# Layer norm and MLP on one core: two token tiles turned by VectorE instead of one, and a narrower first wave of matmuls

## The chip, the cores and the metric

The kernel runs on one core of a Trainium2 chip. A core has five engines that run their own instruction streams and wait for each other by semaphores: TensorE (PE; its weight loads are listed as PEld), VectorE (DVE), ScalarE (ACT), GpSimd (POOL) and SyncE (SP), which here only issues transfers. Tiles lie in the on-chip memory with 128 partitions; matmul results go to eight banks of PSUM, each with 512 float32 columns. The metric is the device time of one execution in microseconds (us), the median of several.

## What is computed

`x` is 2048 tokens by 1024 features, `w1` is 1024 by 3584, `w2` is 3584 by 1024, all in bfloat16:

```
B, S, D, F = 1, 2048, 1024, 3584
y = _layernorm(x, axis=-1)                      # (x - mean) / sqrt(var + eps)
h = _gelu(jnp.einsum("bsd,df->bsf", y, w1) + b1)
return jnp.einsum("bsf,fd->bsd", h, w2) + b2
```

## The kernel before

The tokens are worked on in four blocks of 512, each of four tiles of 128 tokens. For a block, the first product (`mm1`) has 28 rows: row `r` is 128 of the 3584 hidden features, accumulated in one PSUM bank over eight steps `dt` of 128 features, each a matmul of a 128x128 piece of `w1` against 512 token columns of `yT_sb`, the transposed normalized tokens. ACT applies the gelu and writes `hT_sb`. The second product (`mm2`) takes 28 steps for each of its chunks of 512 output columns. A matmul of 512 columns takes 0.216 us, and there are 896 for `mm1` and 896 for `mm2`.

The change is in the start of block 0, while `x` and `w1` arrive. There the first `R = 8` rows of `mm1` are opened early, all eight banks at once, in a "wave": each of the 64 (row, dt) pairs is a cell, one matmul with the piece of `w1` that is there by then. Tiles 0, 1 and 2 are called `RAW`: they go into the wave as they came, not normalized. PE transposes them (`pe_T`, L320 to L356, against an identity), ACT copies the result out of PSUM into buffer 0 of `yT_sb` (L352), and two columns of ones beside them (`N_ONES`) give the column sums of `w1`. ACT copies the negated sums to `ncs` (`put_cs`, L573). Later `ops_fix` (L533) corrects each of the eight rows in PSUM: L536 adds the mean of each token times the column sum, L539 multiplies by the reciprocal standard deviation. For that, means and deviations have to lie along the free dimension: DVE turns them (`ops_row_turn`, L475, L480) and ACT spreads them from the first 32 partitions to the other three groups (`put_row_spread`, L486). `ops_centre` (L523, L529) subtracts the means from the three raw tiles into buffer 1 of `yT_sb`, in four pieces of two `dt`; from row 8 on the matmuls of 512 columns use buffer 1, and only the scaling is left to DVE (L423).

Tile 3 takes another way. DVE takes its statistics (L248, L258), POOL raises the variance to the power -1/2 (L255), DVE normalizes (L262) and transposes it in blocks of 32x32 into `xq_sb` (L490, 1.25 us). Sixteen blocks of 32 partitions then have to move to their places: three by DVE (L498), four by POOL (L495), nine by ACT (L507, `put_moves_3`). Its 64 cells of 128 columns run after the raw wave, row by row; the first waits for all moves, and for the column sums of its row, which its columns overwrite.

The order on each engine is fixed by the order in which the program is written. On DVE it is: statistics of tiles 0, 1, 2; half of the turning of the means; statistics of tile 3; the rest of the turning; normalize, transpose and move tile 3; turn the deviations; centre pieces 0 and 1; fix rows 0 and 1; centre pieces 2 and 3; fix rows 2 to 7. On ACT: copies of the transposed tiles, spreading of the means, column sums of rows in banks 0 to 3, moves of tile 3, two of three spreading copies of the deviations, the other column sums, the last spreading copy, then the gelus. Row 8 reuses the bank of row 0, so it waits for that row's gelu. After the start a planner orders DVE's work for the next blocks by estimated times.

SP issues the loads in one queue in the order of `SP_FIRST_LOADS`. `PIECES` cuts the first 1024 columns of `w1` into nine loads: `(j0, j1, rows)` is the steps `j0` to `j1` for those rows. Rows 0 to 3 come first for all `dt`, then rows 4 to 7; every line of a load is 512 columns, 1024 bytes.

Of the kernel before, what the change touches and what calls it, by code (L numbers as in the profile page):

```python
# [92 lines left out]
def bass_standalone__mixer_channel_mlp__prompt_kernel(  # L93
# [49 lines left out]
    with ExitStack() as es:  # L143
# [176 lines left out]
        def pe_T(i, groups, banks):  # L320
            blk = i // TPB
            src_ev = y_ev[i] if i in y_ev else [x_ev[i][0]] * DT
            evs = yT_ev.setdefault(i, [None] * DT)
            prev = None
            for k, (g0, g1) in enumerate(zip(groups[:-1], groups[1:])):
                bname = banks[k]
                for j in range(g0, g1):
# [8 lines left out]
                    pe.op(lambda e, i=i, j=j, o=off, bap=bank_of[bname]: e.transpose(  # L336
                        out=bap[:, o:o + P], in_=x_sb[:, i, j * P:(j + 1) * P], identity=ident[:, :]),
                        waits=waits, sig=(f"tp{i}_{k}" if last else None))
# [2 lines left out]
            off = 0
            prev = None
            for k, (g0, g1) in enumerate(zip(groups[:-1], groups[1:])):
                bname = banks[k]
                if bname != prev:
                    off = 0
                prev = bname
                done = max(m for m in range(len(banks)) if banks[m] == bname)
                src = bank_of[bname][:, off:off + (g1 - g0) * P].bitcast(I32)
                src = src.rearrange("p (j s) -> p j s", j=g1 - g0)  # L350
                dst = yT_sb[:, 0 if i in RAW else ybuf(blk), g0:g1, ycol(i):ycol(i) + P].bitcast(I32)
                act.op(lambda e, dst=dst, src=src: e.copy(out=dst, in_=src), waits=[f"tp{i}_{done}"],  # L352
                       sig=f"te{i}_{k}")
                off += (g1 - g0) * P
                bank_read[bname] = f"te{i}_{k}"
# [119 lines left out]
        def ops_row_turn(k):  # L475
            res = []
            for tq in range(4):
                src = stat_r[32 * tq:32 * (tq + 1), :, 2 * k:2 * k + 1].to_broadcast([32, len(RAW), 32])
                dst = row_b(k)[0:32, :, 32 * tq:32 * (tq + 1)]
                res.append((lambda e, src=src, dst=dst: e.transpose(out=dst, in_=src),  # L480
                            [("rstd" if k else "mv") + str(t) for t in RAW], (f"row_q{k}" if tq == 3 else None), 0.22))
            return res

        def put_row_spread(k, q0, q1):
            for q in range(q0, q1):
                act.op(lambda e, q=q: e.copy(out=row_b(k)[32 * q:32 * (q + 1)], in_=row_b(k)[0:32]),  # L486
                       waits=[f"row_q{k}"], sig=(f"row_{k}" if q == 3 else None))

        def moves_3():
            res = [(lambda e: e.transpose(out=xq_sb[:, :], in_=x_sb[:, 3, :]), [y_ev[3][-1]], "xq", 1.07)]  # L490
            for tq, q in POOL_MOVES + DVE_MOVES:
                src = xq_sb[32 * tq:32 * (tq + 1), :].rearrange("p (j q s) -> p j q s", j=DT, q=4)[:, :, q, :].bitcast(I32)
                dst = yT_sb[32 * q:32 * (q + 1), ybuf(0), :, ycol(3) + 32 * tq:ycol(3) + 32 * (tq + 1)].bitcast(I32)
                if (tq, q) in POOL_MOVES:
                    pool.op(lambda e, src=src, dst=dst: e.tensor_copy(out=dst, in_=src), waits=["xq"],  # L495
                            sig=("tg3" if (tq, q) == POOL_MOVES[-1] else None))
                if (tq, q) in DVE_MOVES:
                    res.append((lambda e, src=src, dst=dst: e.tensor_copy(out=dst, in_=src), ["xq"],  # L498
                                ("tc3" if len(res) == len(DVE_MOVES) else None), 0.2))
# [2 lines left out]
        def put_moves_3():
            todo = [(tq, q) for tq in range(4) for q in range(4) if (tq, q) not in DVE_MOVES + POOL_MOVES]
            for tq, q in todo:
                src = xq_sb[32 * tq:32 * (tq + 1), :].rearrange("p (j q s) -> p j q s", j=DT, q=4)[:, :, q, :].bitcast(I32)
                dst = yT_sb[32 * q:32 * (q + 1), ybuf(0), :, ycol(3) + 32 * tq:ycol(3) + 32 * (tq + 1)].bitcast(I32)
                act.op(lambda e, src=src, dst=dst: e.copy(out=dst, in_=src), waits=["xq"],  # L507
                       sig=("te3" if (tq, q) == todo[-1] else None))
            yT_ev[3] = ["te3"] * DT
# [42 lines left out]
        pe_T(0, GROUPS_0, ("t", "2_0"))  # L552
        pe_T(1, GROUPS_0, ("2_1", "1_4"))
        pe_T(2, GROUPS_2, ("t", "2_0"))
        put_row_spread(0, 1, 4)
# [8 lines left out]
        first = [(r, dt) for r in PIECES[0][2] for dt in range(*PIECES[0][:2])]  # L564
        for tiles in (RAW[:2], RAW[2:]):
            for r, dt in first:
                wave_cell(r, dt, tiles)
        cells = [(r, dt) for j0, j1, rows in PIECES[1:] for r in rows if r < R for dt in range(j0, j1)]
        for n, (r, dt) in enumerate(cells):
            wave_cell(r, dt, RAW, f"raw_{r}" if dt == DT - 1 else None)  # L570
# [9 lines left out]
        put_cs(0, 4, ps_1[:, 0:4, one0:one0 + 1])  # L580
        put_moves_3()
        put_row_spread(1, 1, 3)
        put_cs(4, NB1, ps_1[:, 4:NB1, one0:one0 + 1])
# [110 lines left out]
```

## Time and profile before

| | |
|---|---|
| median of 3 runs | 396.38 us (396.07, 396.38, 396.78) |
| the profiled execution | 396.67 us, its span 395.4 us |
| PE busy | 390.9 us, 99% of the span |
| DVE, ACT, POOL busy | 162.0, 86.2, 11.7 us |
| transpositions on PE for block 0 | 24, from 3.71 to 6.38 us |
| raw wave, 8 rows by 8 dt | 6.38 to 16.84 us |
| cells of tile 3 | 16.84 to 20.42 us |
| matmuls of 512 columns | from 20.42 us |

Times inside the profile count from the span's first instruction. A line of the timeline gives the start and the duration in us, the engine, the line of the program, the operation, what it writes and reads, how many were merged, and in brackets the idle time before it with what ended it. A matmul is listed from its start until its result is in PSUM, so consecutive ones overlap; the distance of their starts, called the pitch here, is what counts for PE's time. SPq lines are the issue of a transfer, and the view of transfers gives the time from that issue to the landing.

### The profile page before, as it was taken

The numbers are of one execution on the slowest core, as the hardware profiler recorded it, in microseconds if no ns is written. First come the engines' busy times: TensorE is split into PE (matmuls) and PEld (weight loads), VectorE is DVE, ScalarE is ACT, GpSimd is POOL, SyncE is SP. The second block draws the span as 40 slices with busy tenths as digits, with TensorE's granted clock in tenths as the row PEclk, the third lists the DMA queues.
The fourth block names the chain that finished last, engine by engine and source line by source line (L and its number), as shares of the span: only waits on it lengthen the run. The fifth ranks groups of instructions, "written<-read, shape, count | busy, mean of one in ns | idle before, by whom it ended". The sixth has DMA issues, their size and how long they took to land.

```text
span 395.4 us, 4518 instructions
## 1 busy us (share of the span) xinstructions
PE 390.9 (99%) x1904; PEld 184.9 (47%) x1938; DVE 162.0 (41%) x338; ACT 86.2 (22%) x139; POOL 11.7 (3%) x59
## 2 busy tenths in 40 slices
PE   9999999999999999999999999999999999999998
PEld 7744444444444444444444444444444444444444
DVE  5998889988999306987100000001100000001011
ACT  3655420000144332000023443100003334400000
POOL 3101000011001100000000000000000000000000
DMA  7999940000000000000000000000000000000000
GB/s 257 373 385 386 387 155 26 16 27 14 28 0 0 2 0 0 28 26 15 28 13 2 0 0 2 13 13 28 25 15 15 0 0 2 0 15 27 13 28 27
DMA packets 16078, 23.63 MB, mean 60 GB/s; under 512 B 1082, under 2 KB 8250, under 8 KB 16058
## 3 DMA queue, kind: packets, MB, share of 16 engines
q1 hardware_dynamic: 16016, 23.33, 16.7%
q8 instruction: 15, 0.25, 0.3%
q14 instruction: 5, 0.04, 0.0%
q10 hardware_dynamic: 42, 0.01, 0.0%
HBM read 19.14 MB, written 4.19 MB: 59 GB/s over the span
## 4 chain that ended last, share of the span: by engine, by line
PE 99%; issue 0%; DVE 0%
PE ps L449 49%; PE ps L382 38%; PE ps_t L382 7%; PE ps L397 3%; PE ps L471 1%; PE ps_t L397 0%; PE ps L336 0%; PE ps_t L336 0%; DVE o_sb L460 0%; PE ps L512 0%
## 5 line engine op out<-in xcount | busy, mean ns | idle before, releaser
L449 PE MATMUL ps<-w_sb,hT_sb 128*128 128x512 bf16 (+2 forms) x909 | 193.3, 373 | 0.8
L382 PE MATMUL ps<-yT_sb,w_sb 128*128 128x512 bf16 x678 | 152.4, 379 | 0.9
L449 PEld LDWEIGHTS ps<-w_sb,hT_sb 128*128 128x128 bf16 x924 | 88.6, 98 | 105.2
L407 ACT ACTIVATE hT_sb<-ps,b_sb 128x512 bf16<-128x512 f32 x94 | 64.0, 687 | 234.4 <-PE ps L382 217.2
L382 PEld LDWEIGHTS ps<-yT_sb,w_sb 128*128 128x128 bf16 x696 | 68.0, 98 | 81.9
L460 DVE TENSOR_TENSOR o_sb<-ps,b_sb 128x512 bf16<-128x512 f32 (+2 forms) x33 | 22.3, 675 | 198.7 <-PE ps L449 198.5
L304 DVE STREAM_TRANSPOSE yT_sb<-x_sb 32x256 bf16<-32x256 bf16 x192 | 83.7, 436 | 21.9 <-PE ps_t L382 18.8
L382 PE MATMUL ps_t<-yT_sb,w_sb 128*128 128x512 bf16 x135 | 31.9, 379 | 0.1
L248 DVE BATCH_NORM_STATS2 st_sb<-x_sb 128x6 f32<-128x512 bf16 x32 | 21.0, 672 | 4.7 <-DMA x_sb<-in_x_dram 4.6
L382 PEld LDWEIGHTS ps_t<-yT_sb,w_sb 128*128 128x128 bf16 x136 | 13.3, 98 | 16.1
L407 ACT ACTIVATE hT_sb<-ps_t,b_sb 128x512 bf16<-128x512 f32 x18 | 12.4, 687 | 17.5 <-PE ps_t L382 14.6
L397 PE MATMUL ps<-yT_sb,w_sb 128*128 128x128 bf16 (+2 forms) x116 | 13.1, 269 | 0.0
L397 PEld LDWEIGHTS ps<-yT_sb,w_sb 128*128 128x128 bf16 x116 | 8.9, 98 | 3.5
L255 POOL TENSOR_TENSOR rstd_sb<-mv_sb,nhalf 128x1 f32<-128x1 f32 x13 | 7.1, 548 | 113.6 <-DVE mv_sb L258 113.6
L423 DVE TENSOR_TENSOR ps<-ps,row_r 128x384 f32<-128x384 f32 x17 | 9.2, 561 | 2.7 <-PE ps L382 2.5
L262 DVE TENSOR_SCALAR x_sb<-x_sb,mv_sb,rstd_sb 128x1024 bf16<-128x1024 bf16 x13 | 7.0, 541 | 2.0 <-POOL rstd_sb L255 1.3
L536 DVE SCALAR_TENSOR_TENSOR ps<-row_r,ncs,ps 128x384 f32<-128x384 f32 x7 | 4.2, 614 | 0.6 <-PE ps L397 0.6
L486 ACT COPY row_r<-row_r 32x384 f32<-32x384 f32 x6 | 3.1, 510 | 4.3 <-DVE row_r L480 4.2
L539 DVE TENSOR_TENSOR ps<-ps,row_r 128x384 f32<-128x384 f32 x7 | 3.9, 563 | 0.2
L529 DVE TENSOR_TENSOR yT_sb<-yT_sb,row_r 128x768 bf16<-128x768 bf16 x4 | 3.6, 950 | 0.0
L471 PE MATMUL ps<-const-bfloat16-1.0 128*128 128x128 bf16 x25 | 2.8, 309 | 0.8 <-PEq L679 0.8
L258 DVE BATCH_NORM_AGGREGATE mv_sb<-st_sb 128x2 f32<-128x15 f32 x13 | 2.9, 222 | 0.4
(34 smaller groups left out, 32.9 us busy)
## 6 DMA issues: line engine op xcount, KB each, us to landing
w_sb<-in_w_dram SPq DMA_DIRECT2D x4, 1792.0 KB, 18.3
w_sb<-in_w_dram SPq DMA_DIRECT2D x2, 2048.0 KB, 16.4
out_dram<-o_sb SPq DMA_DIRECT2D x31, 128.0 KB, 1.7
x_sb<-in_x_dram SPq DMA_DIRECT2D x3, 1024.0 KB, 14.4
w_sb<-in_w_dram SPq DMA_DIRECT2D x7, 256.0 KB, 5.4
x_sb<-in_x_dram SPq DMA_DIRECT2D x4, 256.0 KB, 3.4
w_sb<-in_w_dram SPq DMA_DIRECT2D x1, 1024.0 KB, 10.1
w_sb<-in_w_dram SPq DMA_DIRECT2D x2, 128.0 KB, 3.7
```

What stands on the lines that cost most here:

```text
L248: return (lambda e, i=i, h=h, pw=pw: e.bn_stats(st_sb[i][:, 6 * h:6 * (h + 1)], x_sb[:, i, h * pw:(h + 1) * pw]), [x_ev[i][h if len(x_ev[i ...
L255: pool.op(lambda e, i=i, dst=dst, mv=mv: e.tensor_tensor(out=dst, in0=mv[:, 1:2], in1=nhalf[:, i:i + 1], op=ALU.pow), waits=[f"mv{i}", "nh ...
L262: return (lambda e, i=i, c0=c0, c1=c1: e.tensor_scalar(out=x_sb[:, i, c0:c1], in0=x_sb[:, i, c0:c1], scalar1=mv_sb[:, i, 0:1], scalar2=rst ...
L304: res.append((lambda e, src=src, dst=dst: e.transpose(out=dst, in_=src), waits, (f"tr{i}" if lastop else None), 0.47))
L382: pe.op(lambda e, b=b, r=r, dt=dt, bank=bank: e.matmul(unit_bank(bank)[:, 0:TB], lhsT=w1_sb[:, dt, r * P:(r + 1) * P], rhs=yT_sb[:, ybuf(b ...
L397: pe.op(lambda e: e.matmul(unit_bank(bank)[:, n0:n1], lhsT=w1_sb[:, dt, r * P:(r + 1) * P], rhs=yT_sb[:, 0 if tiles[0] in RAW else ybuf(0) ...
L407: act.op(lambda e, r=r, n0=n0, n1=n1, bank=bank: e.activation(out=hT_sb[:, r, n0:n1], in_=unit_bank(bank)[:, n0:n1], func=ACT.Gelu_apprx_tanh,
L423: crit.append((est[sig], (lambda e, reg=reg: e.tensor_tensor(out=reg, in0=reg, in1=row_b(1), op=ALU.mult), [sig, "row_1"], ready, 0.57), 0))
L449: pe.op(lambda e, sl=sl, ft=ft, c0=c0, c1=c1, bank=bank: e.matmul(ps_2[:, bank, 0:c1 - c0], lhsT=hT_sb[:, ft, sl * P:(sl + 1) * P], rhs=w2 ...
L460: crit.append((est[sig], (lambda e, ob=ob, c0=c0, c1=c1, bank=bank: e.tensor_tensor(out=o_sb[:, ob, c0:c1], in0=ps_2[:, bank, 0:c1 - c0], ...
L471: pe.op(lambda e: e.matmul(ps_1[:, 0, 0:P], lhsT=ones, rhs=ones, start=True, stop=True))
L536: return [(lambda e: e.scalar_tensor_tensor(out=reg, in0=row_b(0), scalar=ncs[:, c:c + 1], in1=reg, op0=ALU.mult, op1=ALU.add), [f"m1_0_{r ...
```

## The change

- `RAW` is now tiles 0 and 1, and the wave's cells are 258 columns wide (256 and the two of ones). PE transposes 16 pieces, not 24, and each tile's transposed pieces go to two banks of their own, cut after `dt` 1 (`GROUPS`).
- Tiles 2 and 3 (`MADE`) both go the way of tile 3. `xq_sb` has a place for each. Tile 2: DVE moves 1 block, POOL 5, ACT 10. Tile 3: DVE 3, POOL 6, ACT 7. POOL's power for tile 3 waits for POOL's moves of tile 2.
- The 64 raw cells are followed by 64 cells of tile 2 and 64 of tile 3, each of 128 columns. A row's first cell in either waits for its column sums.
- `PIECES` loads `w1` by `dt`: for `dt` 0 rows 0 to 3 and rows 4 to 7 apart, then one load of all eight rows for each `dt`, with 2048 bytes to the line. The wave goes through them in the same order. `x3` is loaded after `w4`, not after `w3`, in loads that are still nine and as large.
- On DVE the order is: statistics of tiles 0 and 2, half of those of tile 1, normalize, transpose and move tile 2, statistics of tile 3, the rest of tile 1, normalize, transpose and move tile 3, turn means and deviations together (4 instructions, not 8), centre pieces 0 and 1, then fix row 0, fix row 1, centre pieces 2 and 3, fix the rest.
- On ACT: copies of the transposed tiles, moves of tile 2, five column-sum copies (there were four), moves of tile 3, spreading of the means, spreading of the deviations, gelus.
- What works on raw tiles (L423, L529, L536, L539, spreading copies) has 256 token columns instead of 384.

```diff
-RAW = (0, 1, 2)
+RAW = (0, 1)
+MADE = (2, 3)
-GROUPS_0 = (0, 4, 8)
-GROUPS_2 = (0, 2, 8)
+GROUPS = (0, 2, 8)
-PIECES = ((0, 1, (0, 1, 2, 3)), (1, 2, (0, 1, 2, 3)), (2, 4, (0, 1, 2, 3)), (4, 6, (0, 1, 2, 3)), (6, 8, (0, 1, 2, 3)),
-          (0, 2, (4, 5, 6, 7)), (2, 4, (4, 5, 6, 7)), (4, 6, (4, 5, 6, 7)), (6, 8, (4, 5, 6, 7)))
+PIECES = ((0, 1, (0, 1, 2, 3)), (0, 1, (4, 5, 6, 7))) + tuple((j, j + 1, tuple(range(8))) for j in range(1, 8))
-DVE_MOVES = ((0, 0), (1, 1), (2, 2))
-POOL_MOVES = ((3, 3), (0, 1), (1, 2), (2, 3))
+POOL_MOVES = {2: 5, 3: 6}
+DVE_MOVES = {2: 1, 3: 3}
-SP_FIRST_LOADS = ("b1", "x0", "x1", "x2", "w0", "w1", "w2", "w3", "x3", "w4", "w5", "w6", "w7", "w8")
+SP_FIRST_LOADS = ("b1", "x0", "x1", "x2", "w0", "w1", "w2", "w3", "w4", "x3", "w5", "w6", "w7", "w8")
...
-                    waits=[f"mv{i}", "nhalf"], sig=f"rstd{i}")
+                    waits=[f"mv{i}", "nhalf"] + ["tg2"] * (i == MADE[1]), sig=f"rstd{i}")
...
+        def ops_moves(i):
+            xq = xq_sb[:, i - MADE[0], :]
+            res = [(lambda e: e.transpose(out=xq, in_=x_sb[:, i, :]), [y_ev[i][-1]], f"xq{i}", 1.25)]
+            np_, nd = POOL_MOVES[i], DVE_MOVES[i]
+            for n, (tq, q) in enumerate(quarters[:np_ + nd]):
+                src, dst = move_aps(i, tq, q)
+                if n < np_:
+                    pool.op(lambda e, src=src, dst=dst: e.tensor_copy(out=dst, in_=src), waits=[f"xq{i}"] + ["rstd1"] * (i == MADE[1]),
+                            sig=(f"tg{i}" if n == np_ - 1 else None))
+                else:
+                    res.append((lambda e, src=src, dst=dst: e.tensor_copy(out=dst, in_=src), [f"xq{i}"],
+                                (f"tc{i}" if n == np_ + nd - 1 else None), 0.23))
...
-        seq = st[0] + st[1] + st[2] + turn_m[:2] + st[3] + turn_m[2:] + nm[3] + moves_3() + turn_r + ctr[:2]
-        for o in seq:
+        for o in st0 + st2 + st1[:1] + nm2 + mv2 + st3 + st1[1:] + nm3 + mv3 + ops_row_turn() + ctr[:2]:
             dve_put(o)
...
+        for j0, j1, rows in PIECES:
+            for r in rows:
+                for dt in range(j0, j1):
+                    wave_cell(r, dt, RAW, f"raw_{r}" if dt == DT - 1 else None)
+        put_moves(2)
...
+        for a, b in ((0, 2), (2, 4), (4, NB1)):
+            put_cs(a, b, ps_1[:, a:b, one0:one0 + 1])
         put_cs(NB1, NB1 + NB2, ps_2[:, 0:NB2, one0:one0 + 1])
         put_cs(NB1 + NB2, R, ps_tf[:, one0:one0 + 1].unsqueeze(1))
+        put_moves(3)
+        put_row_spread(0)
+        put_row_spread(1)
         fixes = []
+        for t in MADE:
+            for r in range(R):
+                for dt in range(DT):
+                    pe_wave(r, dt, (t,), wave[r][0], [cs_ev[r], f"tc{t}", f"tg{t}"] if dt == 0 else [],
+                            f"m1_0_{r}" if t == MADE[-1] and dt == DT - 1 else None)
...
-        for o in [a0, a1, b0, b1_] + ctr[2:] + [o for f in fixes[2:] for o in f]:
+        for o in [a0, b0, a1, b1_] + ctr[2:] + [o for f in fixes[2:] for o in f]:
```

More of the change, by code (lines that the diff above doesn't have):

```diff
@@ L117, in bass_standalone__mixer_channel_mlp__prompt_kernel @@
     assert NB1 + NB2 + 1 <= 8 and NB2 == 2
-    assert all(c[-1] == DT for c in (GROUPS_0, GROUPS_2, HALVES))
-    assert TPB == 4 and RAW == (0, 1, 2)
+    assert all(c[-1] == DT for c in (GROUPS, HALVES))
+    assert TPB == 4 and RAW + MADE == (0, 1, 2, 3)
     w1_chunks = [(j0, j1, rows[0] * P, (rows[-1] + 1) * P) for j0, j1, rows in PIECES]
@@ L159, in bass_standalone__mixer_channel_mlp__prompt_kernel @@
         row_r = sb("row_r", [P, 2 * len(RAW), P], F32)
-        xq_sb = sb("xq_sb", [P, D], BF16)
+        xq_sb = sb("xq_sb", [P, len(MADE), D], BF16)
         ncs = sb("ncs", [P, R], F32)
@@ L340, in pe_T, with put_copy @@
                     off += P
[L341 to L355, printed above, removed]
-            pe_t[0] += DT * 0.056
+            pe_t[0] += DT * 0.056
+        def put_copy(i, groups, banks, k):
+            g0, g1 = groups[k:k + 2]
+            bname = banks[k]
+            assert banks.count(bname) == 1
+            src = bank_of[bname][:, 0:(g1 - g0) * P].bitcast(I32)
+            src = src.rearrange("p (j s) -> p j s", j=g1 - g0)
+            dst = yT_sb[:, 0, g0:g1, ycol(i):ycol(i) + P].bitcast(I32)
+            act.op(lambda e, dst=dst, src=src: e.copy(out=dst, in_=src), waits=[f"tp{i}_{k}"], sig=f"te{i}_{k}")
+            bank_read[bname] = f"te{i}_{k}"
         unit_n = [0]
@@ L389, in pe_wave @@
         def pe_wave(r, dt, tiles, bank, waits, sig):
-            raw = tiles[0] == 0
-            base = raw_at if tiles[0] in RAW else 0
+            raw = tiles == RAW
             y0 = ycol(tiles[0]) - (N_ONES if raw else 0)
-            n0 = base + y0 - ycol(RAW[0]) if tiles[0] in RAW else 0
+            n0 = one0 if raw else (tiles[0] - MADE[0]) * P
             n1 = n0 + ycol(tiles[-1]) + P - y0
@@ L397, in pe_wave @@
             pe.op(lambda e: e.matmul(
-                unit_bank(bank)[:, n0:n1], lhsT=w1_sb[:, dt, r * P:(r + 1) * P], rhs=yT_sb[:, 0 if tiles[0] in RAW else ybuf(0), dt, y0:y0 + n1 - n0],
-                start=(dt == 0 and tiles[0] in (0, 3)), stop=(dt == DT - 1), skip_group_check=True),
+                unit_bank(bank)[:, n0:n1], lhsT=w1_sb[:, dt, r * P:(r + 1) * P], rhs=yT_sb[:, 0 if raw else ybuf(0), dt, y0:y0 + n1 - n0],
+                start=(dt == 0), stop=(dt == DT - 1), skip_group_check=True),
                 waits=w, sig=sig)
@@ L473, in bass_standalone__mixer_channel_mlp__prompt_kernel, with ops_row_turn @@
         warm(N_WARM)
-        def ops_row_turn(k):
+        flat = stat_r[:, :, :].rearrange("p t (k two) -> p (t k) two", two=2)[:, :, 0:1]
+        def ops_row_turn():
             res = []
             for tq in range(4):
[L478 to L481, printed above, removed]
-            return res
@@ L484, in put_row_spread @@
-        def put_row_spread(k, q0, q1):
-            for q in range(q0, q1):
+                src = flat[32 * tq:32 * (tq + 1), :, :].to_broadcast([32, 2 * len(RAW), 32])
+                dst = row_r[0:32, :, 32 * tq:32 * (tq + 1)]
+                res.append((lambda e, src=src, dst=dst: e.transpose(out=dst, in_=src), [f"rstd{t}" for t in RAW],
+                            ("row_q" if tq == 3 else None), 0.31))
+            return res
+        def put_row_spread(k):
+            for q in range(1, 4):
@@ L486, in put_row_spread @@
                 act.op(lambda e, q=q: e.copy(out=row_b(k)[32 * q:32 * (q + 1)], in_=row_b(k)[0:32]),
[L487 to L499, printed above, removed]
-            return res
@@ L502, in put_moves_3 @@
[L502 to L509, printed above, removed]
+                       waits=["row_q"], sig=(f"row_{k}" if q == 3 else None))
@@ new lines, in bass_standalone__mixer_channel_mlp__prompt_kernel, with move_aps @@
+        quarters = [(tq, q) for q in range(4) for tq in range(4)]
+        def move_aps(i, tq, q):
+            src = xq_sb[32 * tq:32 * (tq + 1), i - MADE[0], :].rearrange("p (j q s) -> p j q s", j=DT, q=4)[:, :, q, :].bitcast(I32)
+            dst = yT_sb[32 * q:32 * (q + 1), ybuf(0), :, ycol(i) + 32 * tq:ycol(i) + 32 * (tq + 1)].bitcast(I32)
+            return src, dst
+        def ops_moves(i):
[10 more added lines that the diff above has]
+                                (f"tc{i}" if n == np_ + nd - 1 else None), 0.23))
+            return res
@@ L511, in pe_b1, with put_moves @@
+        def put_moves(i):
+            for tq, q in quarters[POOL_MOVES[i] + DVE_MOVES[i]:]:
+                src, dst = move_aps(i, tq, q)
+                act.op(lambda e, src=src, dst=dst: e.copy(out=dst, in_=src), waits=[f"xq{i}"],
+                       sig=(f"te{i}" if (tq, q) == quarters[-1] else None))
+            yT_ev[i] = [f"te{i}"] * DT
         def pe_b1():
@@ L540, in ops_fix @@
                      [f"fx_a{r}", "row_1"], f"fx_b{r}", 0.42)]
-        st = {i: [op_stats(i, 0), op_stats(i, 1), op_aggr(i)] for i in range(TPB)}
-        nm = {3: ops_norm(3)}
-        turn_m, turn_r = ops_row_turn(0), ops_row_turn(1)
+        stats = lambda i: [op_stats(i, 0), op_stats(i, 1), op_aggr(i)]
+        st0, st2 = stats(0), stats(2)
+        nm2 = ops_norm(2)
+        mv2 = ops_moves(2)
+        st3, st1 = stats(3), stats(1)
+        nm3 = ops_norm(3)
+        mv3 = ops_moves(3)
         ctr = ops_centre()
-        seq = st[0] + st[1] + st[2] + turn_m[:2] + st[3] + turn_m[2:] + nm[3] + moves_3() + turn_r + ctr[:2]
-        for o in seq:
+        for o in st0 + st2 + st1[:1] + nm2 + mv2 + st3 + st1[1:] + nm3 + mv3 + ops_row_turn() + ctr[:2]:
             dve_put(o)
@@ L551, in bass_standalone__mixer_channel_mlp__prompt_kernel @@
         put_b1()
[L552 to L555, printed above, removed]
+        T_BANKS = (("1_4", "2_1"), ("2_0", "t"))
+        for t in RAW:
+            pe_T(t, GROUPS, T_BANKS[t])
+        for k in range(2):
+            for t in RAW:
+                put_copy(t, GROUPS, T_BANKS[t], k)
         wave = [new_unit() for _ in range(R)]
@@ L562, in wave_cell @@
             pe_wave(r, dt, tiles, wave[r][0], waits, sig)
[L564 to L570, printed above, removed]
+        for j0, j1, rows in PIECES:
[3 more added lines that the diff above has]
+        put_moves(2)
         cs_ev = {}
@@ L578, in put_cs @@
                 cs_ev[r] = f"cs{c0}"
[L580 to L583, printed above, removed]
+        for a, b in ((0, 2), (2, 4), (4, NB1)):
+            put_cs(a, b, ps_1[:, a:b, one0:one0 + 1])
         put_cs(NB1, NB1 + NB2, ps_2[:, 0:NB2, one0:one0 + 1])
         put_cs(NB1 + NB2, R, ps_tf[:, one0:one0 + 1].unsqueeze(1))
-        put_row_spread(1, 3, 4)
+        put_moves(3)
+        put_row_spread(0)
+        put_row_spread(1)
         fixes = []
+        for t in MADE:
[3 more added lines that the diff above has]
+                            f"m1_0_{r}" if t == MADE[-1] and dt == DT - 1 else None)
         for r in range(R):
-            for dt in range(DT):
-                pe_wave(r, dt, (3,), wave[r][0], [cs_ev[r], "tc3", "tg3"] if dt == 0 else [],
-                        f"m1_0_{r}" if dt == DT - 1 else None)
             fixes.append(ops_fix(r, wave[r][0]))
```

## The prediction

> **What bounds the kernel now.** I read the page first: who is busy, and who makes the chain that ended last.
>
> ```profile
> PE 390.9 (99%) x1904; PEld 184.9 (47%) x1938; DVE 162.0 (41%) x338; ACT 86.2 (22%) x139; POOL 11.7 (3%) x59
> ...
> PE ps L449 49%; PE ps L382 38%; PE ps_t L382 7%; PE ps L397 3%; PE ps L471 1%; PE ps_t L397 0%; PE ps L336 0%; PE ps_t L336 0%; DVE o_sb L460 0%; PE ps L512 0%
> ```
>
> PE is the bound, and L449 and L382, which the change leaves alone, hold 94% of the chain. From 20.42 us on both kernels issue the same matmuls. So one question is left: when does row 8 start? Next, PE by stage, for the wave's line alone (span, PE busy, clock, transfers).
>
> ```profile
> core 0: us, PE busy (x), PEclk, DMA share, GB/s
> 6.38:6.82 0.44, 0.44 (x4) 1.00 1.29 296
> 7.04:16.84 9.80, 9.80 (x63) 1.00 1.05 354
> 16.84:20.42 3.58, 3.58 (x66) 1.00 1.05 387
> ```
>
> PE never waits in this stage. Four cells of 258 columns in 0.44 us are 0.110 each; 60 cells of 386 in 9.80 are 0.163 (the count takes in neighbours); 64 cells of 128 in 3.58 are 0.056. Third, the transfers: rates by stretch over all engines, then two loads of `w1`, issued at 2.15 and 5.09 us.
>
> ```profile
> 5.00:6.40 1.40, 1.29 (x15) 1.06 (x14) 1.37 (x4) 1.17 (x4) 0.55 (x1) 1.00 1.05 354
> 6.40:8.40 2.00, 2.00 (x20) 1.43 (x18) 1.92 (x6) 0.48 (x1) 0.99 (x2) 1.00 0.94 281
> 8.40:12.70 4.30, 4.30 (x28) 2.59 (x27) 3.49 (x8) 1.45 (x3) 0.66 (x2) 1.00 1.08 362
> 18.00:28.00 10.00, 9.95 (x82) 5.87 (x81) 9.79 (x19) 4.70 (x7) 0.00 (x0) 1.00 1.05 386
> ...
> w_sb<-in_w_dram SPq DMA_DIRECT2D x1, 128.0 KB, 3.8
> ...
> w_sb<-in_w_dram SPq DMA_DIRECT2D x1, 256.0 KB, 5.4
> ```
>
> The last figure of a stretch is GB/s. It dips to 281 between 6.4 and 8.4, is 362 while lines of 1024 bytes come in, and 386 later, with 2048 bytes to the line. `w0` lands at 2.15+3.8 = 5.95 us, `w5` at 5.09+5.4 = 10.5. Last, the work beside PE, from the timeline.
>
> ```profile
> 3.55 1.28 DVE L248 BATCH_NORM_STATS2 st_sb<-x_sb 128x6 f32<-128x512 bf16 x2 [3.55 <-DMA x_sb<-in_x_dram]
> 4.11 1.49 PE L336 MATMUL ps<-ident,x_sb 128*128 128x128 bf16 x12
> ...
> 11.28 0.55 DVE L262 TENSOR_SCALAR x_sb<-x_sb,mv_sb,rstd_sb 128x1024 bf16<-128x1024 bf16 x1
> 11.86 1.25 DVE L490 STREAM_TRANSPOSE xq_sb<-x_sb 128x1024 bf16<-128x1024 bf16 x1
> ...
> 13.14 2.75 ACT L507 COPY yT_sb<-xq_sb 32x128 int32<-32x128 int32 x9 [0.16 <-DVE xq_sb L490]
> 13.14 0.78 DVE L498 COPY yT_sb<-xq_sb 32x128 int32<-32x128 int32 x3
> 13.17 1.33 POOL L495 COPY yT_sb<-xq_sb 32x128 int32<-32x128 int32 x4 [1.93 <-DVE xq_sb L490]
> ...
> 19.14 1.26 ACT L407 ACTIVATE hT_sb<-ps,b_sb 128x512 bf16<-128x512 f32 x2 [1.35 <-DVE ps L539]
> ```
>
> Row 0's gelu ends at about 19.83, 0.6 us before row 8 needs its bank. So DVE and ACT have some room now, but not much.
>
> **PE's work.** Before: 4x0.110 + 4x0.056 + 60x0.163 + 64x0.056 = 14.05 us, from 6.38 to 20.42. After: 64x0.110 + 128x0.056 = 14.20. Splitting tile 2 off costs 0.15 us. Eight transposes and their copies leave: PE ran them from 5.71 to 6.38, straight ahead of the wave. The start now waits for ACT's first two copies, done at about 5.3 (fourth and tenth transposes end near 4.1 and 5.0; 0.27 us a copy), and for `w0`, which lies behind the same three loads of `x` and lands at 5.95. With 0.07 to get going (the wait for a load plus the weight load) the wave starts at 6.02, a gain of 0.36. With no waits PE would reach row 8 at 6.02+14.20 = 20.22, 0.20 earlier than now.
>
> **The loads.** Before, a `dt` of 4 rows is half the bytes in the order used, and a cell is 0.163; now a `dt` is 256 KB for 8 cells of 0.110, 0.88 us, and `x3` comes in between. I take landings by the bytes ahead of them. Loads that complete 1280, 1536, 1792, 2048 and 2304 KB landed at 7.0, 7.9, 9.0, 9.8 and 10.5. In steady flow 256 KB took 0.74 in 1024-byte lines (`w4` to `w8`: 9.8 to 12.7, four loads) and 0.68 in 2048-byte lines (two later loads of 2 MB, landed at 22.7 and 28.1: 5.4/8), so I take 0.07 off for each load of `w1` that has been recut. That gives `dt` 1 at 6.9, `dt` 2 at 7.75, `dt` 3 at 8.8, then `x3` at 9.6, `dt` 4 at 10.2, `dt` 5 at 10.9, `dt` 6 at 11.6, `dt` 7 at 12.3. PE: `dt` 0 6.02 to 6.90; `dt` 1 from 6.98 (wait 0.08); `dt` 2 to 8.74; `dt` 3 from 8.90 (0.16) to 9.78; `dt` 4 from 10.30 (0.52); then three more without a wait, to 13.82. Waits are 0.76. Tile 2's cells then end at 17.40, tile 3's at 20.98: row 8 starts 0.56 later than at 20.42. The bounds of this term: no waits at all (-0.20), or no profit from longer lines and `dt` 4 at 10.5 (+0.86).
>
> One rule speaks against that profit. The Trainium skill, "DMA: Bandwidth & Descriptors", Specifications, gives 512 B as the minimum transfer for line rate, so that 1024 and 2048 bytes to the line would come in alike and the sum would be +0.86. The rates above (362 against 386 GB/s) are nearer to a difference, and I stay with them.
>
> **DVE, ACT and POOL.** Tile 2 now leads DVE's list, and `x2` lands at 1.69+3.9 = 5.6. Statistics 5.6 to 7.1 (1.28+0.22), POOL's power to 7.75 (0.55), normalize 7.8, transpose 8.4 to 9.63, one move to 9.9. Half of tile 1's statistics hides in the wait for POOL. POOL's five moves end at 11.35, ACT's ten (0.306 each) at 12.7: before the 13.82 at which PE wants them, and if that cover went, each ACT move would cost 0.3. Column sums follow the wave by 0.2 (0.17 each); row 0's needs only rows 0 and 1, ready 0.7 before the wave ends. Tile 3: `x3` is in at 9.6, statistics 9.9 to 11.4, rest of tile 1 to 12.25 (it covers POOL's power, which POOL's moves of tile 2 leave free at 11.35), normalize 12.3, transpose 12.9 to 14.1. Moves end: DVE 14.9, POOL 16.2 (six at 0.33), ACT 16.3 (seven). PE wants them at 17.40: hidden, with 1.1 to spare.
>
> Then a chain that before lay beside the wave: turning 4 instructions of 128 columns (96 took 0.28; I take 0.36) to 16.4; six spreading copies. 384 columns took 0.51, 128 took 0.30, so 256 take about 0.41: means at 17.65, deviations at 18.9. Centring two pieces (0.95x2/3, pitch 0.6) to 19.0, fix row 0 (0.62 and 0.56 for 384 columns, 0.49 and 0.43 for 256) to 19.87, gelu 0.69 to 20.6: row 8 could start at 20.7. That is 0.3 ahead of PE's 20.98, so it costs nothing, unless PE is early. Its bounds go from 20.4 (turning at 0.28) to 21.3 (copies at the 0.51 of 384 columns). Centre pieces 2 and 3 end at 21.3 and 21.9, wanted at 21.8 and 22.3. Later rows: a fix took 1.12 us a row and will take about 0.85, so bank releases get no later.
>
> **The sum.** 0.36 gained at the start, 0.15 of split cells, 0.76 of waits: +0.56 (0.55 before rounding) on the profiled execution's 396.67, 397.2. That execution was 0.29 above the median, within the three runs' spread of 0.7. I leave the 0.29 in: the changed start hangs on loads, not on the PE clock's early state.
>
> **Rivals.** *Loads hidden (ends on the other side).* The dip at 6.4 to 8.4 is not the rule: 8.40 to 12.70 has none. Without it (281 instead of 362 for 2 us, 0.45 us) `dt` 4 lands at 9.75 and PE waits 0.1 in all. Then the chain decides, at 20.7: 396.67+0.28 = 396.95; with the chain at its lower bound, 396.65. The point is `dt` 4 before 9.9. For it: packets of the dip need not come again. Against: two stretches before 8.4 already run below 386.
>
> *The chain decides late.* Copies and turning at their upper ends: row 8 at 21.3, 397.5. For it: six copies one after another on ACT, with nothing ahead of them to hide behind.
>
> *The slow pitch lasts.* Transposes ran at a pitch of (1.49-0.31)/11 = 0.107, and from 6.19 on at 0.056, while the granted clock reads 1.00 throughout. PE's gap ahead of the wave grows from 0.32 to 0.6 us. If that keeps PE slow for as long again as the second burst took (3.71 to 6.19, 2.5 us, to 8.7), only 12 cells are done by then and the wave ends at 14.4: +1.1, 397.8. The Trainium skill, "TensorE: Matmul & The Clock Gate", Part 1, says the clock is released after a busy window of about 3.4 us that runs free of the kernel; by that window the pitch would stay slow to 9.6 and the time be 398.2. For it: the gap. Against: PE idled 0.32 before too and the pitch still rose.
>
> *It does not do what it says*, that is, the wave doesn't start earlier, because ACT's copies come later than 5.95: the copies need only four and ten transposes, so I give it no chance of its own.
>
> **How the numbers follow.** A measurement here can tell about 0.2%, 0.8 us: slower begins at 397.17, faster at 395.59. Waits for loads, 397.2 (396.8 to 397.6): 50 in 100, split evenly over that bound, 25 and 25. Loads hidden, 396.95: 23, of which 2 slower. Late chain, 397.5: 13, 12 of them slower. Slow pitch, 397.8: 10, all slower. The last 4 are for faster by 0.2%, which needs row 8 at 19.3 or so, and which I find no mechanism for. Slower 0.49, same 0.47, faster 0.04. The range, 396.5 to 398.0, leaves out 1 in 10 at either end.
>
> **What would show it.** First cell at 6.0; PE idle of 0.4 to 0.6 before `dt` 4, ended by a load; cells of 0.110 and 0.056; tile 2's and tile 3's cells with no gap; row 0's gelu ending before PE's last cell of tile 3. I am wrong if PE's wave has no gap, if a gap stands before row 8 with ACT or DVE as its releaser, or if cells of 258 columns are 0.215 apart.

## The result, and the profile after

The changed kernel takes 397.46 us (median of 11, 397.05 to 398.37) against 396.38 us (11 runs, 396.07 to 397.0): a ratio of 1.0027, 95% interval 1.0018 to 1.0037. Measured again in a later comparison it was 397.62 against 396.69, 1.0021 (1.0009 to 1.0034). So it is slower by 0.2 to 0.3%, some 0.9 to 1.1 us. The forecast was 397.2, 0.8 above the median.

The profiled execution took 397.79 us with a span of 396.6. Its page, the busy engines and the chain that ended last:

```profile
PE 392.3 (99%) x1990; PEld 187.5 (47%) x1990; DVE 157.7 (40%) x337; ACT 87.5 (22%) x146; POOL 13.9 (4%) x66
...
PE 97%; DMA 1%; SPq 1%; issue 0%; DVE 0%
PE ps L442 49%; PE ps L376 38%; PE ps_t L376 7%; PE ps L390 3%; DMA w_sb<-in_w_dram 1%; SPq L188 1%; PE ps_t L390 0%; DVE o_sb L453 0%
```

PE is the bound as before, but a load of `w1` is now in the chain, which was PE to 99% and held no load. (Lines have moved: L390 is the wave's matmul, L376 and L442 the matmuls of 512 columns, L508 the moves, L579 the column sums, L481 the spreading, L400 the gelu.) Who PE waits for between 5 and 22 us (total, times, longest), and PE's and ACT's own lines in the timeline:

```profile
PE ps L390 <- DMA w_sb<-in_w_dram: 1.6, 2, 1.2
```

```profile
6.79 0.93 PE L390 MATMUL ps<-yT_sb,w_sb 128*128 128x258 bf16 x7 [1.18 <-DMA w_sb<-in_w_dram]
7.55 0.27 PE L390 MATMUL ps_t<-yT_sb,w_sb 128*128 128x258 bf16 x1
8.23 0.94 PE L390 MATMUL ps<-yT_sb,w_sb 128*128 128x258 bf16 x7 [0.41 <-DMA w_sb<-in_w_dram]
...
14.40 3.29 PE L390 MATMUL ps<-yT_sb,w_sb 128*128 128x128 bf16 x56
...
17.98 3.29 PE L390 MATMUL ps<-yT_sb,w_sb 128*128 128x128 bf16 x56
...
21.55 1.03 PE L376 MATMUL ps<-yT_sb,w_sb 128*128 128x512 bf16 x4
```

```profile
10.41 3.05 ACT L508 COPY yT_sb<-xq_sb 32x128 int32<-32x128 int32 x10 [4.30 <-DVE xq_sb L493]
14.01 0.72 ACT L579 ACTIVATE ncs<-ps 128x2 f32<-128x2 f32 x4 [0.54 <-PE ps L390]
...
14.81 2.13 ACT L508 COPY yT_sb<-xq_sb 32x128 int32<-32x128 int32 x7
16.97 2.49 ACT L481 COPY row_r<-row_r 32x256 f32<-32x256 f32 x6
20.43 0.69 ACT L400 ACTIVATE hT_sb<-ps,b_sb 128x512 bf16<-128x512 f32 x1 [0.97 <-DVE ps L540]
```

The first cell waits for `w0` and comes at 6.79, 0.4 later than before, not earlier. After eight cells PE waits again for `dt` 1 (starts at 7.55 and 8.23; less the pitch of 0.11 that is 0.57). From there it runs without a gap through the raw wave, tile 2 (14.40) and tile 3 (17.98) to row 8 at 21.55. Row 0's gelu ends at 21.12, so the chain over DVE and ACT is hidden, by 0.4. The loads of `x2`, `w0` and `dt` 1, issued at 1.69, 2.16 and 3.10, took until landing:

```profile
x_sb<-in_x_dram SPq DMA_DIRECT2D x1, 256.0 KB, 4.6
...
w_sb<-in_w_dram SPq DMA_DIRECT2D x1, 128.0 KB, 4.5
...
w_sb<-in_w_dram SPq DMA_DIRECT2D x1, 256.0 KB, 5.1
```

`x2` landed at 6.3 where it was 5.6 in the kernel before, though the loads up to it are the same in both. There its line reads:

```profile
x_sb<-in_x_dram SPq DMA_DIRECT2D x1, 256.0 KB, 3.9
```

A relation holds in all that follows. Time of the profiled execution less the start of row 8: 396.67-20.42 = 376.25 before, 397.79-21.55 = 376.24 after, and 376.24 to 376.32 in eleven of the twelve profiles below. (Five profiles, the kernel before's first among them, lack the record of row 8's first matmul. In four its start follows from the end of the cells ahead of it, which run without a gap; the fifth, which waits there, is the one left out.) The whole difference lies ahead of row 8.

### The profile page after: what moved, and what is told of

Read it like the earlier page. It is cut to its first block, busy times and chain, and to the rows that moved or that the text cites. A ratio compares the mean times of both kernels' runs of the same rounds, so it can differ in the third digit from the quotient of the medians.

```text
span 396.6 us, 4667 instructions
## 1 busy us (share of the span) xinstructions
PE 392.3 (99%) x1990; PEld 187.5 (47%) x1990; DVE 157.7 (40%) x337; ACT 87.5 (22%) x146; POOL 13.9 (4%) x66
## 4 chain that ended last, share of the span: by engine, by line
PE 97%; DMA 1%; SPq 1%; issue 0%; DVE 0%
PE ps L442 49%; PE ps L376 38%; PE ps_t L376 7%; PE ps L390 3%; DMA w_sb<-in_w_dram 1%; SPq L188 1%; PE ps_t L390 0%; DVE o_sb L453 0%
## 5 line engine op out<-in xcount | busy, mean ns | idle before, releaser
L442 PE MATMUL ps<-w_sb,hT_sb 128*128 128x512 bf16 (+2 forms) x924 | 194.1, 373 | 0.0
L376 PE MATMUL ps<-yT_sb,w_sb 128*128 128x512 bf16 x696 | 153.5, 379 | 0.0
L442 PEld LDWEIGHTS ps<-w_sb,hT_sb 128*128 128x128 bf16 x924 | 88.6, 98 | 105.2
L400 ACT ACTIVATE hT_sb<-ps,b_sb 128x512 bf16<-128x512 f32 x94 | 64.3, 688 | 233.2 <-PE ps L376 217.3
L376 PEld LDWEIGHTS ps<-yT_sb,w_sb 128*128 128x128 bf16 x696 | 68.1, 98 | 81.9
L376 PE MATMUL ps_t<-yT_sb,w_sb 128*128 128x512 bf16 x136 | 32.1, 379 | 0.0
L376 PEld LDWEIGHTS ps_t<-yT_sb,w_sb 128*128 128x128 bf16 x136 | 13.3, 98 | 16.0
L400 ACT ACTIVATE hT_sb<-ps_t,b_sb 128x512 bf16<-128x512 f32 x18 | 12.4, 688 | 17.8 <-PE ps_t L376 14.5
L390 PE MATMUL ps<-yT_sb,w_sb 128*128 128x128 bf16 (+1 forms) x168 | 13.7, 237 | 1.6 <-DMA w_sb<-in_w_dram 1.6
L390 PEld LDWEIGHTS ps<-yT_sb,w_sb 128*128 128x128 bf16 x168 | 11.6, 98 | 2.8 <-POOL stat_r L254 1.4
L416 DVE TENSOR_TENSOR ps<-ps,row_r 128x256 f32<-128x256 f32 x17 | 7.1, 431 | 6.1 <-PE ps L376 6.0
L508 ACT COPY yT_sb<-xq_sb 32x128 int32<-32x128 int32 x17 | 5.0, 294 | 4.5 <-DVE xq_sb L493 4.3
L390 PE MATMUL ps_t<-yT_sb,w_sb 128*128 128x128 bf16 (+1 forms) x24 | 3.4, 237 | 0.0
L498 POOL COPY yT_sb<-xq_sb 32x128 int32<-32x128 int32 x11 | 3.2, 295 | 3.2 <-DVE xq_sb L493 2.9
L537 DVE SCALAR_TENSOR_TENSOR ps<-row_r,ncs,ps 128x256 f32<-128x256 f32 x7 | 3.4, 479 | 0.0
```

Of the source, the lines that this page charges most:

```text
L376: pe.op(lambda e, b=b, r=r, dt=dt, bank=bank: e.matmul(unit_bank(bank)[:, 0:TB], lhsT=w1_sb[:, dt, r * P:(r + 1) * P], rhs=yT_sb[:, ybuf(b ...
L390: pe.op(lambda e: e.matmul(unit_bank(bank)[:, n0:n1], lhsT=w1_sb[:, dt, r * P:(r + 1) * P], rhs=yT_sb[:, 0 if raw else ybuf(0), dt, y0:y0 ...
L400: act.op(lambda e, r=r, n0=n0, n1=n1, bank=bank: e.activation(out=hT_sb[:, r, n0:n1], in_=unit_bank(bank)[:, n0:n1], func=ACT.Gelu_apprx_tanh,
L416: crit.append((est[sig], (lambda e, reg=reg: e.tensor_tensor(out=reg, in0=reg, in1=row_b(1), op=ALU.mult), [sig, "row_1"], ready, 0.57), 0))
L442: pe.op(lambda e, sl=sl, ft=ft, c0=c0, c1=c1, bank=bank: e.matmul(ps_2[:, bank, 0:c1 - c0], lhsT=hT_sb[:, ft, sl * P:(sl + 1) * P], rhs=w2 ...
```

## Experiments

Theory L: row 8 is set by PE, which runs ahead of its loads. Theory C: it is set by the chain over DVE and ACT to row 0's gelu. Theory P: the changed program itself makes its early loads late. All runs but two are edits of one line or a few; the ratio is always to the kernel before.

### Both kernels again

No edit.

> The changed kernel, unchanged, for a second profile. Theory L (loads): PE's first cell comes right behind the landing of w0 and the only other wait is for a later load of w1; the two landings move by some tenths of a us between profiles (w0 was at 6.65 us in the first, 5.95 in the kernel before), and the time again is about 397.5 us. Theory C (chain): row 8 begins right behind row 0's gelu, at about 21.1 us, wherever w0 lands. Theory P (the changed program itself makes the early loads late): w0 lands again after 6.5 us.

> The kernel before, unchanged, for a second profile of its loads. Theory L with held-up packets by chance: x2 lands anywhere from 5.6 to 6.3 us here too, and the wave of this kernel, which starts at 6.4 and takes 0.163 us a cell, moves by less than 0.5 us: 396.2 to 396.9. Theory P (the changed program makes its early loads late): x2 lands at 5.6 again.

Measured: the changed kernel 397.62, profile 397.86; the kernel before 396.64 (0.9999, 0.999 to 1.0007), profile 396.98. In the changed kernel's second profile, PE's first cell, and its starts after waits for loads:

```profile
6.71 0.93 PE L390 MATMUL ps<-yT_sb,w_sb 128*128 128x258 bf16 x7 [1.14 <-DMA w_sb<-in_w_dram]
7.47 0.27 PE L390 MATMUL ps_t<-yT_sb,w_sb 128*128 128x258 bf16 x1
7.93 0.94 PE L390 MATMUL ps<-yT_sb,w_sb 128*128 128x258 bf16 x7 [0.18 <-DMA w_sb<-in_w_dram]
...
10.47 0.27 PE L390 MATMUL ps_t<-yT_sb,w_sb 128*128 128x258 bf16 x1
10.93 0.94 PE L390 MATMUL ps<-yT_sb,w_sb 128*128 128x258 bf16 x7 [0.18 <-DMA w_sb<-in_w_dram]
...
21.61 0.60 PE L376 MATMUL ps<-yT_sb,w_sb 128*128 128x512 bf16 x2
```

and ACT's gelu of row 0:

```profile
20.49 0.69 ACT L400 ACTIVATE hT_sb<-ps,b_sb 128x512 bf16<-128x512 f32 x1 [0.97 <-DVE ps L540]
```

Here PE lost 0.35 us ahead of `dt` 1 and 0.35 ahead of `dt` 4. `x2` had landed at 6.23; in the kernel before, run again, at 5.87, and its row 8 began at 20.70. Theory C falls: row 0's gelu ended at 21.17 and row 8 began 0.44 later. Theory P's sign came (`w0` after 6.5, at 6.57), but P is not needed for it: `x2`, behind the same two loads, landed at 5.57, 5.57, 5.64, 5.68, 5.87, 6.04, 6.20, 6.23, 6.29 and 6.32 in ten profiles, and the changed kernel with its variants stands at both ends (5.57 to 6.32), as do two variants of the kernel before (5.64 and 6.20). A narrower form of P is not excluded, though: those two variants also have the new cut of the loads. Sorted by the cut, the three profiles with 1024-byte lines behind `x2` have it at 5.57 to 5.87, and five of the seven with 2048-byte lines at 6.04 or later. Ten profiles are too few to show that the longer lines hold `x2` up, and no experiment here was made for that question.

### No waits for later loads

```diff
+            wd = 0 if raw else dt
-            w.append(f"w1c{w1_chunk_of(r, dt)}")
+            w.append(f"w1c{w1_chunk_of(r, wd)}")
...
-                unit_bank(bank)[:, n0:n1], lhsT=w1_sb[:, dt, r * P:(r + 1) * P], ...
+                unit_bank(bank)[:, n0:n1], lhsT=w1_sb[:, wd, r * P:(r + 1) * P], ...
```

> The changed kernel, but all 64 raw cells take the weights of dt 0, so that the wave waits for w0 and the next load alone (the output is wrong; the matmuls are as many and as wide). Theory L: PE has no gap after the first cells, row 8 could begin 14.2 us after the first cell; if the first cell is at 6.8 that is 21.0, just before row 0's gelu ends (21.1), so 0.3 to 0.6 us less than the changed kernel, 396.9 to 397.2. Theory C: nothing changes, 397.5.

The raw cells leave out the weights of the other seven `dt`; the matmuls are as many and as wide. Measured: 397.19, 1.0021 (1.0009 to 1.0033). Three of its twelve runs stand at 398.5 to 398.7 and the others at 396.25 to 397.52; what set the three apart isn't known. The median is 0.43 under the changed kernel's on that chip, but the ratios' intervals are the same, so the runs do not separate the two. The profile (396.66) does show the mechanism. PE and, below it, ACT:

```profile
13.11 3.29 PE L391 MATMUL ps<-yT_sb,w_sb 128*128 128x128 bf16 x56
...
20.34 0.60 PE L376 MATMUL ps<-yT_sb,w_sb 128*128 128x512 bf16 x2
```

```profile
19.60 0.69 ACT L401 ACTIVATE hT_sb<-ps,b_sb 128x512 bf16<-128x512 f32 x1 [0.97 <-DVE ps L541]
```

`x2` was in at 5.57 and `w0` at 5.93; the first cell came at 6.07, the wave had no gap, tile 2 began at 13.11. PE was through at 20.25, and row 8 began at 20.34, right behind the gelu's end at 20.29. So with no wait for loads the chain is next, at the same place where the kernel before starts row 8 (20.42): even then nothing is gained. In this profile the loads, which are those of the changed kernel, landed at 6.9, 7.8, 8.7 (`dt` 1 to 3), 9.6 (`x3`) and 10.2 (`dt` 4).

### w0 and w1 ahead of x2, with and without later waits

```diff
-SP_FIRST_LOADS = ("b1", "x0", "x1", "x2", "w0", "w1", "w2", ...
+SP_FIRST_LOADS = ("b1", "x0", "x1", "w0", "w1", "x2", "w2", ...
```

> The changed kernel with w0 and w1 loaded before x2. Theory L: w0 lands 0.6 us or more earlier and the first cell follows it, at 5.3 to 6.0, but the load of dt 1 stands where it stood, so PE only waits longer there; x2 comes later by about 0.4 us and the chain behind it too: 397.4 to 397.9. If the late start alone costs the time: 396.7 to 396.9.

> The changed kernel with the weights of dt 0 for all raw cells and with w0 and w1 ahead of x2, so that both waits for loads are out of the way (output wrong; as many matmuls). First cell at 5.4 to 5.6, PE could begin row 8 at 19.7. Theory L with the chain right behind it: PE stands ahead of row 8 until row 0's gelu ends, at 20.7 to 21.3 because x2 is later; 396.9 to 397.5. If the chain has more room than I think: 396.0 to 396.3.

Measured: 397.96 (1.0036, 1.0024 to 1.0048), and 397.89 (1.0022, 1.0009 to 1.0034) with the weights of `dt` 0 throughout. Both lie above the ranges expected for them, the first by 0.06, the second by 0.39. In the first, PE's first cell came at 5.47, 1.3 earlier, and all of it was lost at later loads (0.86, 0.78 and 0.2 us ahead of three of them): row 8 at 21.52. An earlier start alone is worth nothing while the loads behind it stand where they stood. In the second no load holds PE, and two other things do:

```profile
PE ps L391 <- ACT ncs L580: 0.9, 1, 0.9
PE ps L376 <- ACT hT_sb L401: 0.3, 1, 0.3
```

The raw wave was over at 13.1 (its first eight cells took 1.45 us, not 0.88, at a pitch of about 0.2), but ACT was busy with tile 2's moves until 13.96 and the column sums stand behind them; later PE waited for row 0's gelu, which ended at 21.53, after `x2` at 6.81. In the profiles of the changed kernel and of its variants with `x2` behind `x1`, but for the two with a long slow stretch shown below, row 0's gelu ends 14.7 to 14.95 us behind the landing of `x2`. That chain stands close behind PE.

### The place of x3, and of x2

```diff
-..., "w3", "w4", "x3", "w5", ...
+..., "w3", "w4", "w5", "x3", ...
```

```diff
-SP_FIRST_LOADS = ("b1", "x0", "x1", "x2", ...
+SP_FIRST_LOADS = ("b1", "x0", "x2", "x1", ...
```

> The changed kernel with x3 loaded after w5 (dt 4) instead of before it. Theory L: dt 4 lands 0.65 us earlier and PE has no wait there (0.35 us in one of two profiles of the changed kernel); x3 lands at about 10.8, so the chain behind it is up to 0.3 us later: 397.1 to 397.6, row 8 right behind row 0's gelu. If x3's place does not matter: 397.5.

> The changed kernel with x2 loaded before x1. x2 lands at about 4.2 us instead of 5.6 to 6.3, and if row 0's gelu hangs on it (14.7 us later in four profiles) the gelu now ends before 20 us and the chain no longer matters. PE's first cell now waits for tile 1's transposes, at 6.4 to 7.1. Theory L (PE and its loads set row 8): no gain, 397.2 to 397.8. Theory C (the chain set it): 396.4 to 396.9.

Measured: 397.29 (1.0018, 1.0009 to 1.0026) with `x3` later, and 397.56 (1.0025, 1.0016 to 1.0035) with `x2` ahead of `x1`. The first is in the expected range, and too near to the changed kernel to be told from it; its profile is of its slowest run (398.85, with the slow pitch shown below), so it doesn't tell whether the wait ahead of `dt` 4 went. The second settles C again: `x2` landed at 4.16, the gelu ended at 20.73, and row 8 began 0.44 after it, at 21.17, because PE started at 6.58 and waited 0.33 ahead of `dt` 4. ACT's gelu of row 0 and PE's row 8 in it:

```profile
20.05 0.69 ACT L400 ACTIVATE hT_sb<-ps,b_sb 128x512 bf16<-128x512 f32 x1 [0.97 <-DVE ps L540]
```

```profile
21.17 0.59 PE L376 MATMUL ps<-yT_sb,w_sb 128*128 128x512 bf16 x2
```

### The loads cut as before

```diff
-PIECES = ((0, 1, (0, 1, 2, 3)), (0, 1, (4, 5, 6, 7))) + tuple((j, j + 1, tuple(range(8))) for j in range(1, 8))
+PIECES = ((0, 1, (0, 1, 2, 3)), (1, 2, (0, 1, 2, 3)), (2, 4, (0, 1, 2, 3)), ...      # as in the kernel before
-..., "w3", "w4", "x3", "w5", ...
+..., "w3", "x3", "w4", "w5", ...
```

> The changed kernel with the loads of w1 cut and ordered as before (1024 bytes to the line, four rows first, x3 after w3), cells in the order of these loads. If longer lines bring what I took (0.07 us for each load), the wave is behind its loads more often and the kernel is 0.2 to 0.5 us slower than the changed one, 397.7 to 398.0. If the lines make no difference: 397.5.

Measured: 397.85 (1.0035, 1.0023 to 1.0047), inside the range expected if the longer lines bring what was taken. But its profile (398.55) shows another cost, so the median is no clean price of the lines. The transfers tell more. The stretch from 8.4 to 12.7 us, in the changed kernel over all engines and then in this run for PE alone; the last figure is GB/s (362 in the kernel before):

```profile
8.40:12.70 4.30, 4.30 (x41) 3.75 (x40) 4.05 (x8) 2.20 (x8) 2.01 (x7) 1.00 1.03 379
```

```profile
8.40:12.70 4.30, 4.30 (x33) 1.00 1.08 363
```

The last three of the nine loads of `w1` landed 0.74 to 0.76 us apart in the four profiles with 1024-byte lines and 0.65 to 0.73 apart in the ten with 2048. So a profit of about 0.07 a load is there, whatever it does to the time. Stretches of the wave in it, and in the profile with `x3` later (398.85), each for the wave's line alone (span, PE busy, PEld busy, granted clock, transfers):

```profile
6.16:10.20 4.04, 4.04 (x19) 2.82 (x20) 1.00 1.04 348
10.20:15.16 4.96, 4.96 (x46) 4.41 (x45) 1.00 1.09 359
```

```profile
3.70:7.08 3.38, 0.33 (x4) 0.32 (x5) 1.00 0.96 282
7.08:10.46 3.38, 3.38 (x18) 2.36 (x16) 0.51 0.98 352
10.46:15.46 5.00, 5.00 (x47) 4.45 (x46) 0.99 1.08 375
```

In the first, 19 cells took 4.04 us, 0.21 each, and the rest 0.110. In the second, three cells ran at 0.11, then came a stretch of 3.38 us in which the granted clock was 0.51 on average and the pitch 0.21, and then both came back. PE had been busy for 1.44 of the 3.38 us before that. This is the slow pitch of the third rival, and it cost more than the 1.1 us that I gave it: the wave of 64 cells took 8.7 us here and 9.0 there, against 7.04 with no waits. The Trainium skill, "TensorE: Matmul & The Clock Gate", Part 1, states that the clock is decided by activity in a window of 3413 ns that runs free of the kernel; the 3.38 us agrees.

### PE kept busy ahead of the wave

```diff
+        warm(7)
         wave = [new_unit() for _ in range(R)]
```

> The changed kernel with seven more matmuls of 128 columns on ones, between the last transpose and the wave, so that PE is busy while it waits for w0 (0.75 us at a pitch of 0.107). If the slow pitch that one profile of a variant showed for the first 19 cells often strikes the changed kernel, this is faster by 0.3 us or more and its highest runs (398.4) come down: 397.0 to 397.3. If the loads alone set the time (theory L): 397.4 to 397.8.

Measured: 397.47 (1.002, 1.0011 to 1.0028), 396.89 to 397.92. No gain in the median, so the slow pitch is not what makes the typical run of the changed kernel slower; runs near 398.4, of which the changed kernel had two in twenty, are missing here, which eleven runs can't prove. Its profile has `w0` at 6.40, one wait of 0.29 ahead of `dt` 4, and row 8 at 21.03.

### Parts of the change in the kernel before

The cut of the loads alone; the same with the moves ahead of the first column sums; and the early start alone (`w0`, `w1` ahead of `x2`, and the pairs of tiles 0 and 1 for `dt` 0 and 1 ahead of tile 2's transposes).

```diff
-        put_cs(0, 4, ps_1[:, 0:4, one0:one0 + 1])
         put_moves_3()
+        put_cs(0, 4, ps_1[:, 0:4, one0:one0 + 1])
```

```diff
+        first = [(r, dt) for p in PIECES[:2] for r in p[2] for dt in range(*p[:2])]
+        for r, dt in first:
+            wave_cell(r, dt, RAW[:2])
         pe_T(2, GROUPS_2, ("t", "2_0"))
...
+        for r, dt in first:
+            wave_cell(r, dt, RAW[2:])
```

> The kernel before with the new cut of the loads alone (eight rows and 2048 bytes to the line, x3 after w4, cells in that order). Its cells take 0.163 us, so 256 KB serve 1.3 us and come in 0.7: theory L expects no wait for loads, but eight rows end together at the wave's end and the column sums follow it: 396.4 to 396.9. Theory C has no reason for a change either; if this is slower by 0.5 us or more, the cut itself costs something that I don't see.

> The kernel before with the new cut of the loads, as in the run of that cut alone, but ACT's moves of tile 3 stand ahead of the first column-sum copy. If the 2.8 us at tile 3's cells came from the moves standing in ACT's queue behind a copy that waits for rows 0 to 3, the gap goes, row 8 begins at 20.2 to 20.9 and the time is 396.3 to 397.0. If the recut loads cost the time in another way: about 400 again.

> The kernel before with the one part of the change that starts the wave early: w0 and w1 ahead of x2, and the cells of tiles 0 and 1 for dt 0 and 1 of rows 0 to 3 ahead of tile 2's transposes; tile 2 stays raw, the rest as before. First cell at 5.4 to 5.9, PE gains 0.2 to 0.5 us on the kernel before; row 0's gelu (19.8) allows 0.6. Theory L expects 395.9 to 396.3, if x2 is in by 6.6. Theory C (the chain sets the start of row 8 in both kernels): no gain.

Measured: 400.34 (1.0093, 1.0077 to 1.0109), 396.97 (1.0003, 0.9987 to 1.002) and 397.23 (1.0014, 1.0006 to 1.0023). The first was a miss of mine by over 3 us. So was the third, by 0.9: a gain was expected if `x2` came by 6.6. The first one's timeline (of its fastest run, 399.21; the others took up to 401.0, and what they lost beyond it isn't known), ACT and then PE:

```profile
16.31 0.17 ACT L574 ACTIVATE ncs<-ps 128x4 f32<-128x4 f32 x1 [2.75 <-PE ps L396]
16.51 2.74 ACT L506 COPY yT_sb<-xq_sb 32x128 int32<-32x128 int32 x9
```

```profile
19.40 0.77 PE L396 MATMUL ps<-yT_sb,w_sb 128*128 128x128 bf16 x11 [2.55 <-ACT yT_sb L506]
```

With loads by `dt`, rows 0 to 3 end with all the others, so ACT's first column-sum copy waits until 16.31, and the nine moves of tile 3, whose data were ready at 13.89, stand in the queue behind it. PE idles 2.55 us. With the two swapped on ACT, the cost is gone (row 8 at 20.81). So the new cut needs the new order on ACT, which the change has (tile 2's moves ahead of the sums), and the cut by itself is neither gain nor loss for cells of 386 columns. The early start alone lost: tile 2's transposes then waited for `x2`, which landed at 7.0, and PE for their copies; row 8 began at 20.97. None of the variants beats the kernel before.

## Why the prediction was right, and where it was off

**When does row 8 start** was the right question: 376.25 us follow it in both kernels.

**PE's work, 14.20.** From the first cell to row 8 it was 14.76 less a wait of 0.57 in one profile of the changed kernel, 14.90 less 0.70 in the other: 14.19 and 14.20.

**Start at 6.02, a gain of 0.36.** Mis-sized, mostly by the landing of one load. The first cells came at 6.79 and 6.71, since `x2`, and `w0` right behind it, were late; where `x2` was in at 5.57 the variant with `dt` 0's weights started at 6.07. (The 0.07 to get going was 0.13 or 0.14 behind `w0` in every profile in which the first cell waited for it.) Behind the landing of `x2`, the first cell comes after 0.47 or 0.48 in the changed kernel's two profiles and after 0.81 and 0.79 in those of the kernel before. So the gain of a third of a us is there, but both starts hang on a landing that varies by 0.75 us, and I took it from one execution.

**Waits of 0.76, most of it 0.52 ahead of `dt` 4.** They were 0.57 and 0.70, but mostly not where I had them. Place and size differ by profile: 0.57 at `dt` 1; 0.35 and 0.35 at `dt` 1 and 4; 0.29 and 0.33 at `dt` 4 in two variants. `dt` 4 is behind `x3`, as argued, but a late start takes waits from the later loads. The landings of the loads as I had them (6.9, 7.75, 8.8, 9.6, 10.2) are those of one profile with the new cut (`dt` 0's weights) to 0.1; in the changed kernel's own two, `dt` 1 came at 8.19 and 7.89. The bound of +0.86, which takes lines of both lengths to come in alike, falls, since loads with the longer lines landed about 0.07 us closer together.

**The sum, +0.56.** Counted from the landing of `x2`, row 8 began after 14.85 and 14.83 in the kernel before, after 15.23 and 15.38 in the changed one: +0.4 to +0.55. Counted from the span's start it was +1.13 in the first pair of profiles and +0.91 in the second, since `x2` landed 0.75 and 0.36 later in the changed kernel's. The medians differ by 1.08 and 0.93. That leaves some 0.4 us beyond the waits that I summed; in the profiles it is the later `x2`, but unprofiled runs don't show their loads. Whether `x2` is late more often under the changed kernel, or the waits are longer there, stays open. So does whether the new cut makes it late; against a large effect of the cut stands the kernel before with the new cut and the moves first, at 1.0003 (0.9987 to 1.002).

**397.2: in part luck.** The sum was added to a profiled execution 0.29 above the median, and the 0.29 was left in for a reason that no run bears out. The four profiled runs of the two kernels stand 0.29 and 0.34 (before) and 0.33 and 0.24 (changed) above their medians, so in these pairs it cancels. Added to the median, the sum gives 396.94, 0.5 below what was measured; the 0.29 happened to stand in for most of the 0.4 that the sum lacked. The step that fell short is the start: one landing of `x2`, as early as any of the ten, was taken for both kernels.

**DVE, ACT and POOL hidden.** Right: moves of tile 2 ended at 13.46, before the wave's end at 14.4; those of tile 3 at 16.94, wanted at 17.98. The chain's pieces came out as taken (centring pieces at a pitch of 0.61, fixes 0.48 and 0.43, six spreading copies 2.49 in all) or a little better (turning at 0.31 an instruction, 0.36 taken), and it had 0.43 of room, 0.3 forecast.

**Rivals.** Loads hidden: in the variant that takes the waits away the chain decides, as said, and row 8 comes at 20.34 (20.7 said). Late chain: in neither profile. Slow pitch: not in the profiles of the changed kernel, whose waves run at 0.110 after PE gaps of 1.4 us; seen in two variants, at 1.7 to 2 us, and in a third for 0.57.

## What to carry to other kernels

Cells that are made narrower to start sooner also use up their loads sooner: compare the time of one load (0.65 to 0.76 us for 256 KB here) with the matmuls that it feeds (0.88 us now, 1.3 before), and count a load of something else in between as a wait. A start that is moved up to a load's landing takes over that landing's scatter; price it from several profiles. Where loads are reordered, walk each other engine's queue for an early wait that now ends late: one copy of 0.17 us held back 2.7 us of ready moves.

## What the runs showed of the hardware

The same early load, behind the same loads, landed anywhere from 5.57 to 6.32 us. In the late cases (6.04 to 6.32) ten to fourteen of its sixteen parts were in by 5.22 and the rest came after 5.4: in the changed kernel's first profile fourteen were in by 4.99, one at 5.49, the last at 6.32. One late part is enough to hold what waits for the load.

TensorE's clock fell in the middle of the wave in one profile, three cells after PE had come out of 2 us of near idleness, and came back after 3.38 us; the granted clock shows it (0.51). In another profile the pitch was 0.21 for the first 4 us with the granted clock given as 1.00; that trace holds no record of the clock at all, and the view then gives 1.00. The pitch of the matmuls is the safer reading.
